# Residual products in three float32r passes instead of one float32 product

## The chip, the cores and the metric

The kernel runs on one core of one Trainium2 chip. The metric is the time of one execution on the device in microseconds, the median of several runs. Of the kernel before there are three: 1029.36, 1029.59 and 1030.19 us.

## What is computed

The reference takes the real part of a two-dimensional Fourier transform of every batch entry, normalises each row of the result, sends it through two dense layers with a ReLU between them, and adds the row back.

```python
X = np.fft.fft(x, axis=1)            # x: 8 x 3136 x 256
x = np.fft.fft(X, axis=2).real
mu = np.mean(x, axis=-1, keepdims=True)
var = np.mean((x - mu) ** 2, axis=-1, keepdims=True)
xn = (x - mu) / np.sqrt(var + 1e-06) * g_ln
ch = np.maximum(xn @ w_ch1, 0.0) @ w_ch2     # 256 -> 1024 -> 256
out = x + ch
```

All of it is float32. The row `x` that is added at the end is here called the residual.

## The kernel before, in words

The transform along the sequence is split into two steps. Step 1 (`step1`, L244 to L251) multiplies 64-point tables with folded input; its result goes through DRAM and comes back in another layout. Step 2 (`step2`, L298) multiplies that with tables of 98 or 99 columns and leaves in PSUM, for 196 or so frequencies, two sums of 128 rows each (`ps`, 128 x 2 x 196). A row of the transform is a product of these sums with a small table along the feature axis, and this last product is never made for the first dense layer: its table is multiplied into the weights at the start (`transform_w1`), so that the first dense layer works on step 2's sums.

Sums are collected in chunks of 256 frequencies, 49 chunks in all (0 to 48; the last one, `LC`, holds 264 columns). For each chunk step 2's evacuation makes three copies in SBUF:

- `ckh` (L318, ScalarE): the sums rounded to float32r, a format that TensorE multiplies in one pass;
- `ckl` (L322, VectorE): what the rounding left, also float32r;
- `ck` (L320, ScalarE): the sums as plain float32.

The letters of `step2`'s argument say which part runs: "m" the products, "h" the rounded copy, "f" the plain copy, "l" the rest.

A float32 product is then replaced by three float32r products: rest with rounded table, rounded data with the table's rest, rounded with rounded. The dense layers do this throughout (`moe1_a` L342, `moe2` L392). The residual does not: `residual` (L415) multiplies 128 columns of the plain copy `ck`, as the stationary operand, with the float32 table `ty_s` (two halves, of 129 and of 130 columns) into `psy`. That is two instructions to a tile of 128 frequencies and its mirror; there are two tiles to a chunk, four in the last, 100 in all. One tile of the last chunk needs a column set put together from both ends of the chunk (`mixed`, L402 to L404). ScalarE and VectorE then turn `psy` into rows `y` (L422 to L430), take their mean and variance (L437 to L458), and `finish` (L464, L466) adds the dense layers' result.

The main loop runs over s = 6 to 391, eight steps to a chunk. In every step stand, in this order: `moe1_b(s-1)` (ReLU and split, L356 and L357), `moe1_a(s)` (6 products, L342, then L347 to L349), the late list of the step, `moe2(s-3)` (12 products, L392), and the list `after[s]`, in which step 1, step 2 and the residual of chunk c (at s = 8c+5, for chunk 0 at s = 6) are put. The order on the four compute engines is the order in which the program is written; each engine takes its instructions in that order. `residual` writes into the two PSUM buffers `acc` that the chunk before used, so it follows the `finish` of that chunk.

Ahead of the loop stands a start-up part, in which the weights are unpacked from 64-bit numbers (L505 to L568) between the first steps 1 and 2, the tables of step 1 are split into `t1_hi` and `t1_lo`, and the first dense products are made.

Of the kernel before, what the change touches and what calls it, by code (L numbers as in the profile page):

```python
# [20 lines left out]
F32 = mybir.dt.float32  # L21
F32R = mybir.dt.float32r
# [3 lines left out]
ALU = mybir.AluOpType  # L26
# [6 lines left out]
CW = 256  # L33
NCH = -(-NB * REG // CW)
LC = NCH - 1
LASTR = NB * REG - LC * CW
MAXW = LASTR + 2 * NB
# [106 lines left out]
def tile_kernel(ctx: ExitStack, tc: tile.TileContext, x, g_ln, w1, w2, tu, tab, tz, ty, tw, out):  # L144
    nc = tc.nc
    const = ctx.enter_context(tc.tile_pool(name="const", bufs=1))
    work = ctx.enter_context(tc.tile_pool(name="work", bufs=2))
# [8 lines left out]
    tw_s = work.tile([128, 2, 2, 128], F32, tag="o", name="tw_s", bufs=3)  # L156
    ty_s = const.tile([128, 2, 130], F32, name="ty_s")
    g_s = const.tile([128, 2], F32, name="g_s")
    w1_hi = const.tile([128, 2, FF], F32R, name="w1_hi")
    w1_lo = const.tile([128, 2, FF], F32R, name="w1_lo")  # L160
    w2_hi = const.tile([128, 8, D], F32R, name="w2_hi")
# [5 lines left out]
    neg = const.tile([128, 1], F32, name="neg")  # L167
    single = const.tile([128, 2, 2 * NB], F32, name="single")
# [100 lines left out]
    chunk = {}  # L269

    def width(c):
        return MAXW if c == LC else CW

    def first_token(m):
        b, j = divmod(m, 8)
        return b * REG + max(gb[2 * j] - 2, 0)

    def singles():

        full, hi, lo = (t[:, :, LASTR:] for t in chunk[LC])  # L280
        nc.scalar.copy(full, single)
        nc.scalar.copy(hi, single)
        nc.vector.tensor_tensor(out=lo, in0=single, in1=hi.bitcast(F32), op=ALU.subtract)

# [3 lines left out]
    def step2(m, part, of=None):  # L288

        b, j = divmod(m, 8)  # L290
        base, end = gb[2 * j], gb[2 * j + 2]
        if "m" in part:
            ps2[m] = psum.tile([128, 2, CW], F32, tag="y" if m in second else "fft", name=f"ps2_{m}")
        ps = ps2[m]
        for g in (2 * j, 2 * j + 1) if "m" in part else ():
            k0, k1 = gb[g], gb[g + 1]
            for h in range(2):
                nc.tensor.matmul(ps[:, h, k0 - base:k1 - base], s2[b][:KP, g, 128 * h:128 * h + 128],  # L298
                                 tab_s[:, h, k0:k1], start=(h == 0 and g == 2 * j), stop=True,
                                 skip_group_check=True)  # L300
            if g == 0:
                nc.tensor.matmul(ps[:, 1, 0:50], zmu, tz_s, start=False, stop=True,
                                 skip_group_check=True)
        if j == 0 and "f" in part:
            nc.scalar.copy(single[:, :, 2 * b:2 * b + 2], ps[:, :, 0:2])
        t, stop = first_token(m), b * REG + end - 2
        while t < stop:
            c = t // CW
            n = min(stop, c * CW + CW) - t
            if c not in chunk:  # L310
                chunk[c] = (work.tile([128, 2, MAXW], F32, tag="ck", name=f"ck{c}", bufs=3),
                            work.tile([128, 2, MAXW], F32R, tag="ck_hi", name=f"ckh{c}", bufs=3),
                            work.tile([128, 2, MAXW], F32R, tag="ck_lo", name=f"ckl{c}", bufs=3))
            full, hi, lo = (x[:, :, t - c * CW:t - c * CW + n] for x in chunk[c])
            p0 = t - b * REG + 2 - base
            src = ps[:, :, p0:p0 + n]
            if "h" in part and of in (None, c):
                nc.scalar.copy(hi, src)  # L318
            if "f" in part:
                nc.scalar.copy(full, src)  # L320
            if "l" in part and of in (None, c):
                nc.vector.tensor_tensor(out=lo, in0=src, in1=hi.bitcast(F32), op=ALU.subtract)  # L322
            t += n

    PASSES = ((0, 1), (1, 0), (0, 0))
    hh = {}

    def moe1_a(s, passes=((0, 1), (1, 0), (0, 0))):
        c, f = divmod(s, 8)
        w = width(c)  # L330
        ch = chunk[c][1:]
        fs = slice(128 * f, 128 * f + 128)
        wt = (w1_hi, w1_lo)
        if w <= CW:
            ab = psum.tile([128, 2, CW], F32, tag="ab", name=f"ab{s}", bufs=2)
            pa, pb = ab[:, 0], ab[:, 1]
        else:
            pa = psum.tile([128, MAXW], F32, tag="ab", name=f"aa{s}", bufs=2)
            pb = psum.tile([128, MAXW], F32, tag="fft", name=f"bb{s}")
        for j, pt in ((0, pa), (1, pb)):  # L340
            for n, (wi, xi) in enumerate(passes):
                nc.tensor.matmul(pt, wt[wi][:, j, fs], ch[xi][:, j, :w],  # L342
                                 start=(n == 0), stop=(n == 2))
# [5 lines left out]
        nc.vector.tensor_tensor(out=h[:, w:], in0=asb[:, :m], in1=pb[:, :m], op=ALU.subtract)  # L349
# [32 lines left out]
    def moe2(s, halves=((0, 0), (0, 1), (1, 0), (1, 1))):  # L382

        c, f = divmod(s, 8)
        hs = hh[s]
        ws = (w2_hi, w2_lo)
        for i, side in halves:
            if f == 0 and side == 0:
                acc[c, i] = psum.tile([128, 2, D], F32, tag=f"acc{c % 2}", name=f"acc{c}_{i}", bufs=2)
            h0 = 256 * i + 128 * side if c == LC else 128 * i + 256 * side  # L390
            for n, (wi, xi) in enumerate(PASSES):
                nc.tensor.matmul(acc[c, i][:, side], hs[xi][:, h0:h0 + 128], ws[wi][:, f],  # L392
                                 start=(f == 0 and side == 0 and n == 0),
                                 stop=(f == 7 and n == 2), skip_group_check=True)
# [2 lines left out]

    def mixed():

        ck = chunk[LC][0]  # L400
        t = work.tile([128, 2, 128], F32, tag="asb", name="mixed")
        nc.scalar.copy(t[:, :, 0:8], ck[:, :, MAXW - 8:])  # L402
        nc.scalar.copy(t[:, 0, 8:], ck[:, 0, 0:120])
        nc.vector.tensor_scalar(out=t[:, 1, 8:], in0=ck[:, 1, 0:120], scalar1=neg, scalar2=None,  # L404
                                op0=ALU.mult)
        return t

    def residual(c, i):
        last = c == LC and i == 2
        ps = psum.tile([128, 2, 130], F32, tag="y" if last else f"acc{(c + 1) % 2}",  # L410
                       name=f"psy{c}_{i}", bufs=1 if last else 2)
        t0 = 120 if i == 3 else 128 * i
        ck = mixed() if last else chunk[c][0][:, :, t0:t0 + 128]
        for j in range(2):
            nc.tensor.matmul(ps[:, j, :129 + j], ck[:, j], ty_s[:, j, :129 + j],  # L415
                             start=(j == 0), stop=True, skip_group_check=True)
        res[c, i] = ps

    def residual_e(c, i):
# [103 lines left out]
    def split(hi, lo, src, eng=nc.vector):  # L523
        nc.scalar.copy(hi, src)
        eng.tensor_tensor(out=lo, in0=src, in1=hi.bitcast(F32), op=ALU.subtract)
# [55 lines left out]
    def add(s, fn, *args):  # L581

        after.setdefault(s, []).append((fn, args))

    def add_late(s, fn, *args):

        late.setdefault(s, []).append((fn, args))

    first = {}
    for m in range(3, 64):  # L590
        s = 8 * (first_token(m) // CW) - 3
# [2 lines left out]
        first.setdefault(s, []).append(m)  # L594
    for s, ms in first.items():
        for m in ms:
            add(s, step2, m, "mhf")
        for m in ms:
            add_late(s + 1, step2, m, "l")
    for b in range(1, NB):  # L600
# [17 lines left out]
    for c in range(LC):  # L618
        s = 8 * c + (5 if c else 6)
# [26 lines left out]
    with tc.manual_schedule(engines={E.PE, E.Activation, E.DVE, E.Pool}):  # L646
        with tc.manual_schedule(engines={E.SP}):
# [70 lines left out]
            for i in range(NU):  # L718
# [5 lines left out]
            f = finish_w2(0)  # L724
# [5 lines left out]
            step2(1, "m")  # L730
            step2(1, "hl", 0)
            moe1_a(0, ((1, 0), (0, 0), (0, 1)))
            step2(0, "f")
            convert_a("w2_1", w2p[1])
            moe1_a(1, ((1, 0), (0, 0), (0, 1)))
            convert_b("w2_1")
# [8 lines left out]
            step2(1, "f")  # L745
            step2(1, "hl", 1)
            moe2(0)
            convert_a("w2_2", w2p[2])
# [5 lines left out]
            f = finish_w2(2)  # L754
# [3 lines left out]
            moe1_a(5)  # L758
            moe1_b(4)
            convert_b("w2_3")  # L760
            step2(2, "hf")
            step2(2, "l")
            moe2(2)
            split(t1_hi, t1_lo, tu_s[:, 0:128])
            add_late(6, make_w2, 3)

        main.append(True)
        lag, last = 3, 8 * NCH
# [33 lines left out]
```

## Time and profile before

| what | value |
|---|---|
| median of three runs | 1029.59 us |
| the profiled execution's own time | 1029.71 us |
| its span in the trace | 1027.9 us |
| mean granted TensorE clock | 0.997 |
| TensorE busy | 1008.6 us, 98% of the span |
| VectorE busy | 816.0 us, 79% |
| ScalarE busy | 539.7 us, 53% |
| GpSimd busy | 245.0 us, 24% |

The span is the stretch between the first and the last instruction of the trace; 1.8 us of the execution's time lie around it. Names of tiles are printed without buffer numbers. A float32 product stands in the trace as two pairs of a weight load (PEld) and a matmul (PE), a float32r product as one such pair. The shape behind a matmul is rows x moving columns; "128*128" is the stationary tile. In the timeline a row is start, duration, engine, line and operation, and like instructions that follow each other are merged ("x8"). Matmuls overlap in the pipeline, so the distance between starts, not the duration, says what one costs.

### The profile page before, as it was taken

What the parts mean: (1) busy time and instruction counts of PE and PEld (TensorE: products, weight loads), DVE (VectorE), ACT (ScalarE), POOL (GpSimd) and SP (SyncE); (2) the same over time, 40 slices, a digit from 0 to 9 for tenths busy, and PEclk for the clock granted to TensorE, in tenths of its full rate; (3) what the DMA queues carried; (4) which work ended last, traced back from release to release, by engine and by line L of the source; (5) the groups of instructions that cost most, each with busy time, mean ns of one, the idle gap of its engine ahead of it and who ended that gap; (6) DMA issues with size and microseconds to landing.
All of it is one profiled execution on the core that took longest, in us unless ns stands there. A gap on an engine that the chain in (4) does not pass through costs nothing.

```text
span 1027.9 us, 21753 instructions
## 1 busy us (share of the span) xinstructions
PE 1008.6 (98%) x8282; PEld 986.0 (96%) x8283; DVE 816.0 (79%) x2195; ACT 539.7 (53%) x1410; POOL 245.0 (24%) x277
## 2 busy tenths in 40 slices
PE   9799999999999999999999999999999999999997
PEld 6489999999999999999999999999999999999997
DVE  5788787778878878887887887878788778788787
ACT  2445555554465555555455545654555554455553
POOL 1146503440135202532034401442024300000000
PEclk9999999999999999999999999999999999999999
DMA  9923341423222331234114132223101230100101
GB/s 332 263 98 128 109 134 52 135 83 103 66 99 87 108 94 42 94 102 135 43 62 144 63 103 82 84 93 114 62 24 51 73 103 22 42 22 21 42 22 42
DMA packets 41528, 92.04 MB, mean 90 GB/s; under 512 B 4176, under 2 KB 18704, under 8 KB 40528
## 3 DMA queue, kind: packets, MB, share of 16 engines
q1 hardware_dynamic: 40016, 88.81, 26.4%
q8 instruction: 66, 1.08, 0.5%
q0 software_dynamic: 320, 1.05, 0.3%
q10 hardware_dynamic: 1088, 0.79, 0.2%
q14 instruction: 38, 0.31, 0.1%
HBM read 50.26 MB, written 40.37 MB: 88 GB/s over the span
## 4 chain that ended last, share of the span: by engine, by line
PE 93%; DVE 5%; ACT 1%; issue 0%; DVEq 0%; ACTq 0%
PE acc L392 51%; PE ab L342 26%; PE ps L298 5%; PE psy L415 4%; PE ps L251 3%; DVE h_lo L357 1%; PE pw L643 1%; DVE h L348 1%; DVE h L349 1%; PE ps L244 1%; PE ps L246 1%; ACT h_hi L356 0%; DVE ew L520 0%; PE psw L558 0%; DVE fw L507 0%
## 5 line engine op out<-in xcount | busy, mean ns | idle before, releaser
L392 PE MATMUL acc<-w_hi,h_lo 128*128 128x256 f32 x1568 | 438.9, 280 | 2.8 <-DVE h_lo L357 2.8
L392 PE MATMUL acc<-w_hi,h_hi 128*128 128x256 f32 x1568 | 439.1, 280 | 0.0
L392 PE MATMUL acc<-w_lo,h_hi 128*128 128x256 f32 x1568 | 438.8, 280 | 0.0
L357 DVE SCALAR_TENSOR_TENSOR h_lo<-h,h_hi 128x512 fp32r<-128x512 f32 x392 | 287.9, 735 | 174.1 <-ACT h_hi L356 172.3
L356 ACT ACTIVATE h_hi<-h 128x512 fp32r<-128x512 f32 x392 | 249.8, 637 | 254.2 <-DVE h L349 253.9
L392 PEld LDWEIGHTS acc<-w_hi,h_lo 128*128 128x128 f32 x1568 | 295.6, 189 | 3.3 <-DVE h_lo L357 3.2
L392 PEld LDWEIGHTS acc<-w_lo,h_hi 128*128 128x128 f32 x1568 | 295.5, 188 | 0.0
L392 PEld LDWEIGHTS acc<-w_hi,h_hi 128*128 128x128 f32 x1568 | 295.4, 188 | 0.0
L342 PE MATMUL ab<-ckl,w_hi 128*128 128x256 f32 x768 | 220.9, 288 | 3.7 <-DVE h L349 3.7
L342 PE MATMUL ab<-ckh,w_lo 128*128 128x256 f32 x768 | 216.0, 281 | 0.4 <-ACT ckh L318 0.4
L342 PE MATMUL ab<-ckh,w_hi 128*128 128x256 f32 x768 | 214.8, 280 | 0.0
L214 POOL TENSOR_TENSOR fl<-f,fh 128x512 fp32r<-128x512 f32 x49 | 64.8, 1321 | 506.9 <-ACT fh L208 506.9
L348 DVE TENSOR_TENSOR h<-asb,ab 128x256 f32<-128x256 f32 x384 | 158.8, 414 | 2.2 <-ACT asb L347 2.2
L349 DVE TENSOR_TENSOR h<-asb,ab 128x256 f32<-128x256 f32 x384 | 158.9, 414 | 0.0
L342 PEld LDWEIGHTS ab<-ckl,w_hi 128*128 128x128 f32 x768 | 144.5, 188 | 7.2 <-ACT ye L423 1.7
L347 ACT COPY asb<-ab 128x256 f32<-128x256 f32 x384 | 139.3, 363 | 18.7 <-PE ab L342 12.9
L342 PEld LDWEIGHTS ab<-ckh,w_lo 128*128 128x128 f32 x768 | 145.0, 189 | 2.6 <-ACT ckh L318 0.5
L342 PEld LDWEIGHTS ab<-ckh,w_hi 128*128 128x128 f32 x768 | 145.1, 189 | 0.0
L254 ACT COPY s<-ps 128x508 f32<-128x508 f32 x56 | 32.7, 585 | 82.9 <-PE ps L251 65.4
L318 ACT CAST ckh<-ps 128x392 fp32r<-128x392 f32 (+49 forms) x112 | 39.6, 355 | 66.0 <-PE ps L298 65.7
L298 PE MATMUL ps<-tab_s,s 112*128 112x98 f32 (+1 forms) x512 | 66.4, 275 | 0.1
L298 PEld LDWEIGHTS ps<-tab_s,s 112*128 112x128 f32 x512 | 63.0, 194 | 0.6 <-PE pw L643 0.6
(108 smaller groups left out, 964.9 us busy)
## 6 DMA issues: line engine op xcount, KB each, us to landing
xs<-x SPq DMA_DIRECT2D x56, 512.0 KB, 4.6
out<-o SPq DMA_DIRECT2D x96, 256.0 KB, 3.0
scratch<-s SPq DMA_DIRECT2D x49, 256.0 KB, 2.2
s<-scratch SPq DMA_DIRECT2D x7, 1792.0 KB, 9.9
w1p_all<-w SPq DMA_DIRECT2D x8, 512.0 KB, 8.7
scratch<-s POOLq DMA_DIRECT2D x4, 256.0 KB, 6.0
s<-scratch SPq DMA_DIRECT2D x2, 448.0 KB, 5.9
s<-scratch SPq DMA_DIRECT2D x1, 896.0 KB, 11.7
```

What stands on the lines that cost most here:

```text
L214: nc.gpsimd.tensor_tensor(out=lo, in0=f, in1=hi.bitcast(F32), op=ALU.subtract)
L254: nc.scalar.copy(s[:, :, :, :127], ps[:, :, :, :127])
L298: nc.tensor.matmul(ps[:, h, k0 - base:k1 - base], s2[b][:KP, g, 128 * h:128 * h + 128], tab_s[:, h, k0:k1], start=(h == 0 and g == 2 * j), ...
L318: nc.scalar.copy(hi, src)
L342: nc.tensor.matmul(pt, wt[wi][:, j, fs], ch[xi][:, j, :w], start=(n == 0), stop=(n == 2))
L347: nc.scalar.copy(asb[:, :w], pa)
L348: nc.vector.tensor_tensor(out=h[:, :w], in0=asb[:, :w], in1=pb, op=ALU.add)
L349: nc.vector.tensor_tensor(out=h[:, w:], in0=asb[:, :m], in1=pb[:, :m], op=ALU.subtract)
L356: nc.scalar.activation(h_hi, h, AF.Relu)
L357: nc.vector.scalar_tensor_tensor(out=h_lo, in0=h, scalar=0.0, in1=h_hi.bitcast(F32), op0=ALU.max, op1=ALU.subtract)
L392: nc.tensor.matmul(acc[c, i][:, side], hs[xi][:, h0:h0 + 128], ws[wi][:, f], start=(f == 0 and side == 0 and n == 0), stop=(f == 7 and n = ...
L415: nc.tensor.matmul(ps[:, j, :129 + j], ck[:, j], ty_s[:, j, :129 + j], start=(j == 0), stop=True, skip_group_check=True)
```

## The change

The residual's product is made as the dense layers make theirs: the table `ty_s` is split once into `ty_hi` and `ty_lo`, and each half of each tile is multiplied in three float32r passes from `ckl` and `ckh`. Both halves now have 130 columns. The plain copy `ck` is no longer made: all "f" parts of `step2` go, 112 ScalarE copies, one more in `singles`, and a pool of three buffers. `mixed` now builds a rounded and a remaining tile, with twice the copies. In the start-up part one `split` of the table is added.

```diff
+    ty_hi = const.tile([128, 2, 130], F32R, name="ty_hi")
+    ty_lo = const.tile([128, 2, 130], F32R, name="ty_lo")
...
     def singles():
-        full, hi, lo = (t[:, :, LASTR:] for t in chunk[LC])
-        nc.scalar.copy(full, single)
+        hi, lo = (t[:, :, LASTR:] for t in chunk[LC])
...
             if "h" in part and of in (None, c):
                 nc.scalar.copy(hi, src)
-            if "f" in part:
-                nc.scalar.copy(full, src)
...
     def mixed():
-        ck = chunk[LC][0]
-        t = work.tile([128, 2, 128], F32, tag="asb", name="mixed")
-        nc.scalar.copy(t[:, :, 0:8], ck[:, :, MAXW - 8:])
-        nc.scalar.copy(t[:, 0, 8:], ck[:, 0, 0:120])
-        nc.vector.tensor_scalar(out=t[:, 1, 8:], in0=ck[:, 1, 0:120], scalar1=neg, scalar2=None,
-                                op0=ALU.mult)
-        return t
+        out = []
+        for ck, tag in zip(chunk[LC], ("f_hi", "f_lo")):
+            t = work.tile([128, 2, 128], F32R, tag=tag, name=f"mixed_{tag}")
+            nc.scalar.copy(t[:, :, 0:8], ck[:, :, MAXW - 8:].bitcast(F32))
+            nc.scalar.copy(t[:, 0, 8:], ck[:, 0, 0:120].bitcast(F32))
+            nc.vector.tensor_scalar(out=t[:, 1, 8:], in0=ck[:, 1, 0:120].bitcast(F32), scalar1=neg,
+                                    scalar2=None, op0=ALU.mult)
+            out.append(t)
+        return out
...
     def residual(c, i):
-        ck = mixed() if last else chunk[c][0][:, :, t0:t0 + 128]
+        ck = mixed() if last else [x[:, :, t0:t0 + 128] for x in chunk[c]]
         for j in range(2):
-            nc.tensor.matmul(ps[:, j, :129 + j], ck[:, j], ty_s[:, j, :129 + j],
-                             start=(j == 0), stop=True, skip_group_check=True)
+            for n, (ti, xi) in enumerate(PASSES):
+                nc.tensor.matmul(ps[:, j], ck[xi][:, j], (ty_hi, ty_lo)[ti][:, j],
+                                 start=(j == 0 and n == 0), stop=(n == 2), skip_group_check=True)
...
-            add(s, step2, m, "mhf")
+            add(s, step2, m, "mh")
...
-            step2(2, "hf")
+            step2(2, "h")
             step2(2, "l")
             moe2(2)
+            split(ty_hi, ty_lo, ty_s)
             split(t1_hi, t1_lo, tu_s[:, 0:128])
```

`PASSES` is ((0, 1), (1, 0), (0, 0)), pairs of table and data with 0 for rounded and 1 for the rest. What the change does to the order on the engines is seen at three places.

On TensorE, the residual of chunk 1 before (`ps_3` is step 2, `psy_0` and `psy_1` are the two tiles, `ab` is the first dense layer of the next step):

```order
L298 MATMUL ps_3_814<-tab_s,s_0_260 128x98 x4
L415 MATMUL psy_0_827<-ty_s,ck_335 128x129
L415 MATMUL psy_0_827<-ty_s,ck_335 128x130
L415 MATMUL psy_1_830<-ty_s,ck_335 128x129
L415 MATMUL psy_1_830<-ty_s,ck_335 128x130
L342 MATMUL ab_837<-ckl_337,w_hi 128x256
```

The same place now, from step 2 to the first product of the second tile (line numbers of the changed file):

```order
L299 MATMUL ps_3_818<-tab_s,s_0_262 128x98 x4
L416 MATMUL psy_0_828<-ty_hi,ckl_338 128x130
L416 MATMUL psy_0_828<-ty_lo,ckh_337 128x130
L416 MATMUL psy_0_828<-ty_hi,ckh_337 128x130
L416 MATMUL psy_0_828<-ty_hi,ckl_338 128x130
L416 MATMUL psy_0_828<-ty_lo,ckh_337 128x130
L416 MATMUL psy_0_828<-ty_hi,ckh_337 128x130
L416 MATMUL psy_1_835<-ty_hi,ckl_338 128x130
```

Two instructions of a tile have become six, at the same place between step 2 and the dense products.

On VectorE, the end of the start-up part before (`ckl` is the rest of step 2's sums, `t_lo` the rest of step 1's table, `h_lo` the ReLU's rest in step 6):

```order
L520 SCALAR_TENSOR_TENSOR ew_3_479<-w1p_all,ew_3_479 128x512
L322 TENSOR_TENSOR ckl_337<-ps_2_456,ckh_336 128x2x121
L322 TENSOR_TENSOR ckl_463<-ps_2_456,ckh_462 128x2x75
L525 TENSOR_TENSOR t_lo<-tu_s,t_hi 128x128
L357 SCALAR_TENSOR_TENSOR h_lo_525<-h_493,h_hi_524 128x512
```

and now:

```order
L521 SCALAR_TENSOR_TENSOR ew_3_475<-w1p_all,ew_3_475 128x512
L320 TENSOR_TENSOR ckl_338<-ps_2_453,ckh_337 128x2x121
L320 TENSOR_TENSOR ckl_459<-ps_2_453,ckh_458 128x2x75
L526 TENSOR_TENSOR ty_lo<-ty_s,ty_hi 128x260
L526 TENSOR_TENSOR t_lo<-tu_s,t_hi 128x128
L355 SCALAR_TENSOR_TENSOR h_lo_521<-h_489,h_hi_520 128x512
```

One operation of 260 columns, `ty_lo`, has come in ahead of `t_lo`; the residual of chunk 0 reads it.

On ScalarE, the evacuation of two steps 2 that feed chunks 3 and 4, before (`ckh` the rounded, `ck` the plain copy, `h_hi` the ReLU of the next step):

```order
L318 CAST ckh_822<-ps_4_1148 128x2x196
L320 COPY ck_821<-ps_4_1148 128x2x196
L318 CAST ckh_822<-ps_5_1155 128x2x45
L320 COPY ck_821<-ps_5_1155 128x2x45
L318 CAST ckh_1163<-ps_5_1155 128x2x151
L320 COPY ck_1162<-ps_5_1155 128x2x151
L356 ACTIVATE h_hi_1174<-h_1132 128x512
```

and now:

```order
L345 COPY asb_1140<-ab_1133 128x256
L318 CAST ckh_824<-ps_4_1157 128x2x196
L318 CAST ckh_824<-ps_5_1163 128x2x45
L318 CAST ckh_1169<-ps_5_1163 128x2x151
L354 ACTIVATE h_hi_1187<-h_1141 128x512
```

The three plain copies are gone, and the ReLU follows the last rounded copy.

More of the change, by code (lines that the diff above doesn't have):

```diff
@@ L303, in step2 @@
                                  skip_group_check=True)
-        if j == 0 and "f" in part:
+        if j == 0 and "h" in part:
             nc.scalar.copy(single[:, :, 2 * b:2 * b + 2], ps[:, :, 0:2])
@@ L310, in step2 @@
             if c not in chunk:
-                chunk[c] = (work.tile([128, 2, MAXW], F32, tag="ck", name=f"ck{c}", bufs=3),
-                            work.tile([128, 2, MAXW], F32R, tag="ck_hi", name=f"ckh{c}", bufs=3),
+                chunk[c] = (work.tile([128, 2, MAXW], F32R, tag="ck_hi", name=f"ckh{c}", bufs=3),
                             work.tile([128, 2, MAXW], F32R, tag="ck_lo", name=f"ckl{c}", bufs=3))
-            full, hi, lo = (x[:, :, t - c * CW:t - c * CW + n] for x in chunk[c])
+            hi, lo = (x[:, :, t - c * CW:t - c * CW + n] for x in chunk[c])
             p0 = t - b * REG + 2 - base
@@ L330, in moe1_a @@
         w = width(c)
-        ch = chunk[c][1:]
+        ch = chunk[c]
         fs = slice(128 * f, 128 * f + 128)
@@ L732, in tile_kernel @@
             moe1_a(0, ((1, 0), (0, 0), (0, 1)))
-            step2(0, "f")
             convert_a("w2_1", w2p[1])
@@ L744, in tile_kernel @@
             moe1_a(3)
-            step2(1, "f")
             step2(1, "hl", 1)
```

## Prediction

> **What bounds the kernel now.** I began with the page: busy time of each engine, then the chain that ended last.
>
> ```profile
> PE 1008.6 (98%) x8282; PEld 986.0 (96%) x8283; DVE 816.0 (79%) x2195; ACT 539.7 (53%) x1410; POOL 245.0 (24%) x277
> ...
> PE 93%; DVE 5%; ACT 1%; issue 0%; DVEq 0%; ACTq 0%
> ```
>
> TensorE is busy for 98% of the span, and 93% of the chain lies on it. Next come the waits of TensorE over the whole run: who held it up, the total in microseconds, how often, and the longest.
>
> ```profile
> PE ab L342 <- DVE h L349: 3.7, 6, 1.5
> ...
> PE ab L342 <- ACT ckh L318: 0.4, 1, 0.4
> ```
>
> The longest total is 3.7 us, and ScalarE is named once, with 0.4. Hardly any of it lies in the body of the run: from 83 to 993 us, by the table of windows, TensorE is busy for 908.94 of 910 us, against 730.71 on VectorE and 491.79 on ScalarE.
>
> ```profile
> 83.00:993.00 910.00, 908.94 (x7654) 902.35 (x7654) 730.71 (x1992) 491.79 (x1289) 224.90 (x246) 1.00 0.25 80
> ```
>
> So in the body of the run each stretch that the change adds to TensorE is paid in full, and what it takes from ScalarE is paid out nowhere, unless TensorE waits for ScalarE there. The question is what a residual tile costs on TensorE in six narrow float32r pairs instead of four narrow float32 pairs. A pair is a weight load and a matmul; matmuls overlap in the pipeline, so a duration isn't a price, and I go by distances between starts. The timeline of the weight loads around the residual of one chunk (two tiles, eight loads) has them:
>
> ```profile
> 401.94 0.97 PEld L415 LDWEIGHTS psy<-ty_s,ck 128*128 128x128 f32 x8
> 402.83 0.19 PEld L342 LDWEIGHTS ab<-ckl,w_hi 128*128 128x128 f32 x1
> 402.94 0.19 PEld L342 LDWEIGHTS ab<-ckh,w_lo 128*128 128x128 f32 x1
> ```
>
> Eight pairs take 402.83 - 401.94 = 0.89 us, 0.111 us each, and a tile of four pairs 0.445 us.
>
> **What a narrow float32r pair will cost.** No row of this trace has a float32r product of fewer than 256 columns, so the price is bounded from both sides. First the moving columns. The chain shows the 18 dense pairs of a step, float32r with 256 columns; the timeline shows step 1's products with 512 (fl, fh):
>
> ```profile
> 98.15 0.71 PE ab L342 x6
> 98.86 1.42 PE acc L392 x12
> ```
>
> ```profile
> 409.95 0.39 PE L251 MATMUL ps<-fl,t_hi 128*128 128x512 f32 x1
> 410.18 0.39 PE L251 MATMUL ps<-fh,t_lo 128*128 128x512 f32 x1
> ```
>
> 256 columns take (0.71 + 1.42)/18 = 0.118 us, 512 take 410.18 - 409.95 = 0.23: the time goes with the columns. For 130 that makes 130/256 x 0.118 = 0.060 us. That is the low end, if columns alone count. Now the loads. Here are the products of step 1's ends, float32, with 14 moving columns (L226, L227) or a single one (L230):
>
> ```profile
> 407.07 0.30 PEld L226 LDWEIGHTS pse<-e0c,tu_s 128*128 128x128 f32 x2
> 407.29 0.30 PEld L227 LDWEIGHTS pse<-e0c,tu_s 128*128 128x128 f32 x2
> 407.52 0.28 PEld L230 LDWEIGHTS pse<-one,masked 128*112 128x112 f32 x2
> 407.71 0.19 PEld L342 LDWEIGHTS ab<-ckl,w_hi 128*128 128x128 f32 x1
> ```
>
> Two loads with 14 columns behind them take 0.22 us, as long as two with 129. With 112 stationary columns instead of 128 two take 0.19. So in a row of narrow products it is the weight load that sets the pace, at 0.11 us for 128 stationary columns, however few columns move. For float32r there are two places where a load isn't held back by a wide matmul ahead of it: the first load of `ab` after the residual, 402.83 to 402.94, 0.11 us, and the warm-up's first two:
>
> ```profile
> 7.22 0.19 PEld L643 LDWEIGHTS pw<-warm_r 128*128 128x128 f32 x1 [0.89 <-PE pw L643]
> ...
> 7.33 0.19 PEld L643 LDWEIGHTS pw<-warm_r 128*128 128x128 f32 x1
> ```
>
> Again 0.11. A float32r load therefore costs what a float32 load does, and I take 0.111 us for the pair: the load's pace, not the columns' 0.060. The nearest float32r pairs, of 256 columns, give 0.118 as the upper end of this case.
>
> **The change part by part.**
>
> *Six pairs instead of four.* Two more pairs of 0.111 us are 0.222 us a tile. (That the first half gains a 130th column changes nothing at this pace.) There are 100 tiles, and for four of them it is not all on the path. Chunk 0's two stand in the start-up stretch, and chunk 1's first tile ahead of a wait of TensorE:
>
> ```profile
> 58.36 1.05 PE L415 MATMUL psy<-ty_s,ck 128*128 128x129 f32 x8
> ...
> 80.63 0.71 PE L415 MATMUL psy<-ty_s,ck 128*128 128x129 f32 x4 [1.63 <-DVE o L466]
> ```
>
> What comes ahead of 80.63 has 1.63 us of wait to spare there. The fourth is the tile from `mixed`, below. The other 96 are paid in full: 96 x 0.222 = 21.3 us. With 0.109 and 0.118 for a pair (the first is 0.002 less, what two decimals of such distances leave open) the ends are 96 x (0.654 - 0.445) = 20.1 and 96 x (0.708 - 0.445) = 25.2.
>
> *The wait for ty_lo.* The residual of chunk 0 will need the table's rest, which VectorE makes late, ahead of `t_lo`:
>
> ```profile
> 60.25 0.28 DVE L525 TENSOR_TENSOR t_lo<-tu_s,t_hi 128x128 fp32r<-128x128 f32 x1
> 60.45 0.69 DVE L357 SCALAR_TENSOR_TENSOR h_lo<-h,h_hi 128x512 fp32r<-128x512 f32 x1
> ```
>
> 128 columns take 0.20 us there from start to start; an estimate for 260 is 0.3, between that and the 0.69 that the 512 columns of the second row last. VectorE leads the chain in this stretch, so 0.3 us goes on the path. TensorE stood at this product at 58.36 and will now wait, after its first pair, until about 60.6. Queued behind are the 11 other pairs (1.2 us) and the dense products of the next step (0.71 for `ab`, 1.42 for `acc`, as above), which end at 63.9 instead of 58.36 + 0.89 + 0.71 + 1.42 = 61.4: 2.5 us late. The waits that TensorE has between 60 and 82 us are the cover:
>
> ```profile
> PE ab L342 <- DVE h L349: 2.3, 4, 1.5
> PE psy L415 <- DVE o L466: 1.6, 1, 1.6
> ```
>
> They make 3.9 us, more than 2.5. I cost the stall at nothing; if that cover weren't there, for example because VectorE in turn waits for the late `ab`, it would be up to 2.5 us.
>
> *The plain copies go.* 112 copies leave ScalarE, 40.3 us:
>
> ```profile
> L320 ACT COPY ck<-ps 128x392 f32<-128x392 f32 (+49 forms) x112 | 40.3, 364 | 0.0
> ```
>
> In the body this meets a wait of TensorE once. The chain between 80 and 130 us shows it: copies, ReLU, and the rest `ckl` one after another, then step 1's product, which waits for the last `ckl`; the timeline has that wait.
>
> ```profile
> 101.18 0.49 ACT ckh L318
> 101.67 0.39 ACT ck L320
> 102.45 0.31 ACT ckh L318
> 102.76 0.32 ACT ck L320
> ...
> 104.99 1.02 DVE ckl L322 x3
> ```
>
> ```profile
> 106.15 0.48 PE L251 MATMUL ps<-fl,t_hi 128*128 128x512 f32 x1 [1.06 <-DVE ckl L322]
> ```
>
> Two plain copies are 0.39 + 0.32 = 0.7 us of it, and chunk 2's residual, which runs on TensorE beside them, takes 0.44 us of the wait as well. Together that is the whole 1.1 us: -1.1. Everywhere else the copies are hidden behind TensorE already, and they bring nothing.
>
> *The tail.* `mixed` gets two more ScalarE copies and one more VectorE operation, and TensorE waits there already:
>
> ```profile
> 1002.45 0.40 PE L415 MATMUL psy<-ty_s,mixed 128*128 128x129 f32 x2
> 1003.28 0.49 PE L415 MATMUL psy<-ty_s,mixed 128*128 128x130 f32 x2 [0.43 <-DVE mixed L404]
> ```
>
> The second operation takes 0.2 us (`t_lo`'s start to start), and of the two new pairs one, of the second half, comes after it: 0.1. Together 0.3. The last `ck` copy in `singles` goes: 0.1 less.
>
> *Sum.* 21.3 + 0.3 - 1.1 + 0.3 - 0.1 = 20.7 us. The profiled execution took 1029.71 us, 1.8 above its span and 0.12 above the median of the three; on it this makes 1050.4. A difference of 0.2%, 2 us, is about what a measurement of this kernel can tell from none.
>
> **The rivals.**
>
> *The load is not the limit (faster).* If float32r pairs of 130 columns ran at their columns' pace, a tile would take 6 x 0.060 = 0.36 us instead of 0.445, and 96 tiles would give 8.2 us back: 1020.9 with the other terms (-0.6). The point at which this decides is a pair of 0.445/6 = 0.074 us: below it the change gains. For it: loads overlap, with 0.19 us of duration every 0.11. Against it: the rows with 14 columns and with one, which would have run far below 0.11 if columns counted. Chance 0.05. Just at 0.074 nothing changes (within 0.2%): 0.02.
>
> *The load is hidden in part.* A pair halfway between, at 0.085 us, makes 0.51 us a tile, 0.065 more: 6 us, 1035.4. Against it the same rows, all at 0.11. Chance 0.04. The Trainium skill (TensorE: Matmul & The Clock Gate, "Back-to-back issue gap") gives about 81 ns for each pair in a sustained stream with 128 moving columns; by that rule the time would be an estimate of 1033 us. The loads of this trace, 0.11 us apart with 14 columns, so far speak against it for four-byte operands.
>
> *Narrow float32r takes more passes.* Nothing here shows float32r below 256 columns, and it could need several passes of its columns. Two passes are 0.12, the upper end above. Four are 0.24 us a pair, 1.44 a tile, 0.995 more: 96 tiles make 95.5 us, 1124.6 with the other terms. It decides from about 0.12 on, where columns overtake the load. For it speaks only that this program has no such product; against it, that the time went with the columns from 256 to 512 without a step. Chance 0.09.
>
> *As forecast*, with the load's pace: 0.80.
>
> **Numbers.** The likeliest case gives 1050.4 us. Its ends are 1029.7 + 20.1 - 1.1 - 0.1 = 1048.6 and 1029.7 + 25.2 + 0.6 = 1055.5; I go to 1047.5 below, since the plain copies' end might be worth another microsecond in the start-up stretch. The range 1047.5 to 1055.5 leaves out the rivals at 1021, 1035 and 1125 us, 2 in 10 in all. Faster 0.05, same 0.02, slower 0.93 (0.80 + 0.09 + 0.04).
>
> **What the profile of the changed kernel would show.** Twelve loads of `psy` to a chunk in 1.33 us, 0.111 from start to start, and 200 more matmuls and loads on the page. TensorE's share stays at 98%; ScalarE's busy time falls by some 40 us, to about 500. At 58 us `psy` waits about 2 us for `ty_lo`, and the wait at 80.6 nearly vanishes. No wait for `ckl` is left at 106. The forecast is wrong if `psy`'s loads stand at 0.06 to 0.09 us or the matmuls at 0.24, or if the loss comes from new waits instead of from twelve loads.

## The result, and the profile after

The kernel after takes 1054.57 us (median of six runs, 1054.15 to 1056.30), the kernel before beside it 1029.89 us (six runs, 1029.36 to 1031.58). The ratio is 1.0238, with a 95% interval of 1.0225 to 1.0252. The direction and the mechanism came as forecast, and the time lies inside the range; it is 4.2 us above the 1050.4 that was held likeliest. The profiled execution took 1054.17 us, 24.46 more than that of before, where the steps summed to 20.7. So there are 20 us to confirm, and 3.8 us to find.

The page of the kernel after, its busy times, its granted clock in 40 slices and its chain:

```profile
PE 1034.8 (98%) x8482; PEld 1012.3 (96%) x8483; DVE 818.8 (78%) x2197; ACT 509.8 (48%) x1300; POOL 243.7 (23%) x277
...
PEclk9989999999999999999999999999999999999999
...
PE 94%; DVE 5%; ACT 1%; issue 0%; ACTq 0%; DVEq 0%
```

There are 200 more matmuls and 200 more loads, as expected, and TensorE stays at 98%. ScalarE falls by 29.9 us (539.7 to 509.8), not by the 40 expected: the 40.3 us were the sum of the durations of 112 copies, and durations of instructions that follow each other closely overlap, so the busy time on the page loses less than the group's row shows. Nobody waited for ScalarE, so this costs the forecast nothing. New is the 8 in the third slice of the clock (53 to 79 us).

The timeline of the weight loads of the kernel after, around the residual of one chunk (twelve loads of `psy`, then the first of `ab`):

```profile
410.72 0.19 PEld L416 LDWEIGHTS psy<-ty_hi,ckl 128*128 128x128 f32 x1
410.83 0.19 PEld L416 LDWEIGHTS psy<-ty_lo,ckh 128*128 128x128 f32 x1
...
411.95 0.19 PEld L416 LDWEIGHTS psy<-ty_hi,ckh 128*128 128x128 f32 x1
412.06 0.19 PEld L340 LDWEIGHTS ab<-ckl,w_hi 128*128 128x128 f32 x1
```

From 410.72 to 412.06 are 1.34 us for twelve, 0.112 each (forecast 1.33 and 0.111). Eight loads took 0.89 before. That is 0.45 us a chunk.

To see where the other microseconds lie, I compare the starts of the same products in both traces: one in step 0, the first `ab` of step 15, and the first `aa` of the last chunk (step 384). The timeline of the matmuls before:

```profile
40.19 0.36 PE L342 MATMUL ab<-ckl,w_hi 128*128 128x256 f32 x1
...
83.28 0.28 PE L342 MATMUL ab<-ckl,w_hi 128*128 128x256 f32 x1
...
998.07 0.28 PE L342 MATMUL aa<-ckl,w_hi 128*128 128x264 f32 x1
```

The same three in the timeline after:

```profile
40.69 0.36 PE L340 MATMUL ab<-ckl,w_hi 128*128 128x256 f32 x1
...
85.07 0.28 PE L340 MATMUL ab<-ckl,w_hi 128*128 128x256 f32 x1
...
1021.71 0.28 PE L340 MATMUL aa<-ckl,w_hi 128*128 128x264 f32 x1
```

The distances grow from 0.50 to 1.79, 23.64 and, at the end, 24.46 us. By stretch, with the terms of the forecast sorted into the same stretches:

| stretch | forecast | measured |
|---|---|---|
| to step 0 | 0 | 0.50 |
| step 0 to 15 | 0.3 + 0.22 = 0.5 | 1.29 |
| step 15 to 384, residuals of 46 chunks | 92 x 0.222 - 1.1 = 19.3 | 21.85 |
| from there to the end | 3 x 0.222 + 0.3 - 0.1 = 0.9 | 0.82 |
| sum | 20.7 | 24.46 |

The first 0.50 us lie ahead of everything that the change touches: nearly all of them are there already in the first eight products of zeros with which TensorE warms up. The chain before, and then after:

```profile
1.49 5.69 PE pw L643 x8
```

```profile
1.49 6.18 PE pw L644 x8
```

Two stretches remain, with 0.8 and 2.5 us.

**Step 0 to 15.** The waits of TensorE over the whole run after:

```profile
PE psy L416 <- DVE ty_lo L526: 2.1, 1, 2.1
...
PE psy L416 <- DVE o L467: 1.5, 2, 1.2
PE ps L253 <- DVE ckl L320: 1.0, 1, 1.0
PE ab L340 <- DVE h L347: 0.8, 1, 0.8
```

The wait for `ty_lo` is there, 2.1 us. The waits for `h` shrank from 3.7 to 0.8 us and those for `o` from 3.0 to 1.5: they are the cover on which the forecast counted, and they are used up. The timeline of the matmuls after shows why they did not suffice:

```profile
58.87 0.22 PE L416 MATMUL psy<-ty_hi,ckl 128*128 128x130 f32 x1
61.20 0.47 PE L416 MATMUL psy<-ty_lo,ckh 128*128 128x130 f32 x1 [2.11 <-DVE ty_lo L526]
61.48 0.41 PE L416 MATMUL psy<-ty_hi,ckh 128*128 128x130 f32 x1
61.69 0.41 PE L416 MATMUL psy<-ty_hi,ckl 128*128 128x130 f32 x1
```

After the wait the pairs stand 0.21 us apart, not 0.11. The table of windows after, where the column ahead of the DMA share and the GB/s is the granted clock:

```profile
62.00:66.00 4.00, 4.00 (x20) 4.00 (x20) 2.78 (x5) 1.83 (x5) 1.99 (x2) 0.50 0.00 0
66.00:70.00 4.00, 4.00 (x29) 4.00 (x28) 2.38 (x7) 1.62 (x6) 3.91 (x6) 0.76 0.35 117
```

And the same table before:

```profile
62.00:66.00 4.00, 2.47 (x20) 2.30 (x21) 2.43 (x4) 2.58 (x8) 2.79 (x4) 1.00 0.00 0
```

In these four microseconds TensorE starts as many matmuls as before, 20, but is busy for 4.00 us instead of 2.47, at a clock of 0.50.

**Step 15 to 384.** The wait at 106 us, which the forecast let vanish with the plain copies (-1.1), is still there: 0.99 us at 108.27. The chain of the kernel after at that place:

```profile
102.02 1.76 PE ps L299 x16
103.78 1.32 PE psy L416 x12
105.10 0.78 PE ab L340 x6
...
105.96 0.38 ACT asb L345
...
106.36 0.42 DVE h L346
106.78 0.33 DVE h L347
107.11 1.02 DVE ckl L320 x3
...
108.27 0.93 PE ps L253 x3
```

Before, the copies of ScalarE stood between `ps` and `ckl` in the chain. Now the chain reaches `ckl` by way of `h` on VectorE, and the input of `h`, `ab`, is made by TensorE itself, after the residual: TensorE waits for work that its own longer residual has put back. The rest of the stretch, 2.55 - 1.1 = 1.4 us, has no wait beside it. It lies in the dense products: twelve loads of `moe2` take a mean of 1.4016 us before and 1.4075 after, from the starts of the first load of a group and the one that follows its last, over all groups between 120 and 985 us, at a granted clock of 1.00 in both.

### The profile page after: what moved, and what is told of

It is laid out like the page before. It is cut to its first block, busy times and chain, and to the rows that moved or that the text cites. A ratio compares the mean times of both kernels' runs of the same rounds, so it can differ in the third digit from the quotient of the medians.

```text
span 1052.4 us, 22045 instructions
## 1 busy us (share of the span) xinstructions
PE 1034.8 (98%) x8482; PEld 1012.3 (96%) x8483; DVE 818.8 (78%) x2197; ACT 509.8 (48%) x1300; POOL 243.7 (23%) x277
## 4 chain that ended last, share of the span: by engine, by line
PE 94%; DVE 5%; ACT 1%; issue 0%; ACTq 0%; DVEq 0%
PE acc L390 50%; PE ab L340 25%; PE psy L416 6%; PE ps L299 5%; PE ps L253 3%; PE pw L644 1%; DVE h_lo L355 1%; DVE h L346 1%; DVE h L347 1%; PE ps L246 1%; PE ps L248 0%; DVE ew L521 0%; PE psw L559 0%; DVE fw L508 0%; ACT asb L345 0%
## 5 line engine op out<-in xcount | busy, mean ns | idle before, releaser
L318 ACT CAST ckh<-ps 128x392 fp32r<-128x392 f32 (+49 forms) x112 | 34.2, 350 | 72.1 <-PE ps L299 72.1
```

## The experiments

**Theory.** In a row of narrow products the weight load sets the pace, 0.111 us for 128 stationary columns whatever moves; a float32r pass of the residual costs that, and everything else is small change (the clock after the wait for `ty_lo`, the copies). **First rival:** the moving columns, or the float32r passes over them, set the price. **Second rival:** a good part of the loss comes from the new wait for `ty_lo` with its half clock, so that an early table gives it back. Ratios below are to the kernel before, on the same chip.

### Half the moving columns

The second and third pass move 64 columns instead of 130.

```diff
-                nc.tensor.matmul(ps[:, j], ck[xi][:, j], (ty_hi, ty_lo)[ti][:, j],
+                k = 130 if n == 0 else 64
+                nc.tensor.matmul(ps[:, j, :k], ck[xi][:, j], (ty_hi, ty_lo)[ti][:, j, :k],
```

> The changed kernel with the second and third pass of each product made for the first 64 of the 130 moving columns only; the other columns keep the first pass alone. Theory (the weight load sets the pace of a pair): loads of psy stay 0.111 us apart, 1054 us, within 1 us of the changed kernel. Rival (moving columns count): 66 columns less at 0.118/256 us each are 0.030 us a pair, four such pairs to a tile, 98 tiles: 12 us less, 1042.

It took 1054.35 us (1052.34 to 1056.13), ratio 1.0235 (1.0214 to 1.0256). The loads of a chunk in its timeline, the first of `psy` and the first of `ab` behind it:

```profile
411.03 0.19 PEld L417 LDWEIGHTS psy<-ty_hi,ckl 128*128 128x128 f32 x1
...
412.37 0.19 PEld L340 LDWEIGHTS ab<-ckl,w_hi 128*128 128x128 f32 x1
```

Still 1.34 us for twelve. The moving columns cost nothing here, and the first rival is out. The Trainium skill (TensorE: Matmul & The Clock Gate, "Back-to-back issue gap") gives about 81 ns for a pair in a stream with 128 moving columns; this trace has 112 with 130 and with 64, and differs.

### Half the stationary columns

The same two passes load 64 stationary columns instead of 128.

```diff
-                nc.tensor.matmul(ps[:, j], ck[xi][:, j], (ty_hi, ty_lo)[ti][:, j],
+                k = 128 if n == 0 else 64
+                nc.tensor.matmul(ps[:k, j], ck[xi][:, j, :k], (ty_hi, ty_lo)[ti][:, j],
```

> The changed kernel with the second and third pass of each product made for 64 of the 128 stationary columns only; the other rows of the tile keep the first pass alone. Theory (the time to load stationary columns sets the pace): 16 columns less were worth 0.016 us on the products of step 1's ends, so 64 columns load in about 0.05 us, and the 130 moving columns, 0.06 us, become the limit: four pairs of a tile save 0.05 us each, 98 tiles, 20 us less, 1034. Rival (a fixed price for each pair, however much is loaded): no change, 1054.

It took 1033.18 us (1032.68 to 1035.75), ratio 1.0039 (1.0025 to 1.0054). Its loads, with the stationary columns as the second number of 128*64:

```profile
402.54 0.19 PEld L417 LDWEIGHTS psy<-ty_hi,ckl 128*128 128x128 f32 x1
402.65 0.14 PEld L417 LDWEIGHTS psy<-ty_lo,ckh 128*64 128x64 f32 x1
402.71 0.14 PEld L417 LDWEIGHTS psy<-ty_hi,ckh 128*64 128x64 f32 x1
402.78 0.19 PEld L417 LDWEIGHTS psy<-ty_hi,ckl 128*128 128x128 f32 x1
...
403.48 0.19 PEld L340 LDWEIGHTS ab<-ckl,w_hi 128*128 128x128 f32 x1
```

A pass with half the load costs 0.06 us, one with the whole 0.11, and the chunk 0.94 instead of 1.34. The same number of products, with the same 130 moving columns, is 21.4 us faster than the kernel after (1054.57 - 1033.18), most of the loss. The price goes with the stationary columns, and a fixed price for each pair is out. What half a load costs by itself the run doesn't show: its 0.06 us are also what the prediction estimated for 130 moving columns (0.060). (The Trainium skill, same page, "LDWEIGHTS (loading the stationary operand)", lets a load grow with its columns, at 1.2 columns a nanosecond. By it the two loads would take 107 and 53 ns; the 0.11 agrees, and the 0.06 is an upper bound for the second.)

### Two passes

The pass of the data's rest with the rounded table is left out.

```diff
-            for n, (ti, xi) in enumerate(PASSES):
+            for n, (ti, xi) in enumerate(PASSES[1:]):
...
-                                 start=(j == 0 and n == 0), stop=(n == 2), skip_group_check=True)
+                                 start=(j == 0 and n == 0), stop=(n == 1), skip_group_check=True)
```

> The changed kernel without the first of the three passes (the rest of the data with the rounded table): four float32r pairs to a tile where the kernel before had four float32 pairs. Theory (a pair costs the load of 128 stationary columns, whatever its type): the time of the kernel before plus what the start-up part keeps, 0.6 us without and 1.4 us with a drop of the clock there: 1030 to 1031.5, within 0.2% of the kernel before in the same call. Rival (float32r pairs have a price of their own, for example a larger one for narrow products): 4 pairs x 98 tiles x the difference, 4 us or more for each 0.01 us.

It took 1032.22 us (1030.38 to 1033.40), ratio 1.0016 (1.0005 to 1.0028), 0.7 above the upper edge of what was expected. Eight loads of float32r with the plain copies gone take 0.89 us a chunk, the same as the eight of the float32 product before: two passes of float32r cost what one float32 product costs. The ten executions fall apart by the mean clock that was granted to each: the six at 0.993 or 0.994 have a median of 1032.6 us, the four at 0.997 one of 1030.6. The profiled one is of the first kind, with a clock of 0.62 from 62 to 66 us, after a wait for `ty_lo` of 2.2 us.

### One load for two passes

If the load is the price, a pass that shares a load should be nearly free. Here the rounded data is loaded once for 256 moving columns, 130 of the rounded table and 126 of its rest, and the data's rest once for 130. The table is split early. The sums with the table's rest land in columns of their own and aren't added.

```diff
...
-                nc.tensor.matmul(ps[:, j], ck[xi][:, j], (ty_hi, ty_lo)[ti][:, j],
-                                 start=(j == 0 and n == 0), stop=(n == 2), skip_group_check=True)
+            nc.tensor.matmul(ps[:, j], ck[0][:, j], ty_both[:, j],
+                             start=(j == 0), stop=False, skip_group_check=True)
+            nc.tensor.matmul(ps[:, j, :130], ck[1][:, j], ty_hi[:, j],
+                             start=False, stop=True, skip_group_check=True)
```

> The three products with one load of the rounded data less: the rounded table and 126 columns of its rest stand side by side, and the rounded data, loaded once, is multiplied with all 256 columns; the rest of the data follows with 130 columns. The sums with the table's rest stand in columns of their own and are not added, so two additions to a tile are left out. The split stands early, as in the kernel with the early split. Theory (price by loads, or by columns where they are more): a tile is 2 x 0.118 + 2 x 0.111 = 0.458 us against 0.445 before, 98 tiles make 1.3 us, with the start-up part's 0.6 about 2 us above the kernel before, 1031.5 to 1032.5, and some 21 us below the changed kernel. Rival (a price for each of the three products, however loaded): no better than the changed kernel, 1053.

It took 1032.28 us (1031.97 to 1035.02), ratio 1.0027 (1.0014 to 1.0041), as expected. All three products of a tile are made (of the table's rest 126 of 130 columns), with eight loads to a chunk; its timeline:

```profile
402.61 0.19 PEld L415 LDWEIGHTS psy<-ty_both,ckh 128*128 128x128 f32 x1
402.73 0.19 PEld L417 LDWEIGHTS psy<-ty_both,ckl 128*128 128x128 f32 x1
...
403.54 0.19 PEld L340 LDWEIGHTS ab<-ckl,w_hi 128*128 128x128 f32 x1
```

0.93 us a chunk: of two passes that share a load the second costs (0.93 - 0.89)/4 = 0.01 us.

### The table split early

The split of the table is moved ahead of the late start-up work, its rest made on GpSimd.

```diff
             moe1_b(3)
+            split(ty_hi, ty_lo, ty_s, nc.gpsimd)
...
-            split(ty_hi, ty_lo, ty_s)
             split(t1_hi, t1_lo, tu_s[:, 0:128])
```

> The changed kernel, but the table's split stands some 8 us earlier in the start-up part, and its rest is made on GpSimd, which is idle there. Nothing waits for ty_lo then. Theory: the wait of 2.1 us at 59 us in the changed kernel also brought the granted clock down to half from 62 to 68 us, and the dense products of that stretch ran at 0.213 us a pair; both go. 1.0 to 1.5 us less than the changed kernel, about 1053.2, a clock of 1.00 in all windows from 58 to 82 us, and a wait of psy at about 81 us again. Rival: the cover of 3.9 us absorbs the stall as the prediction had it: no gain beyond the 0.3 us of the VectorE operation, 1054.2.

It took 1052.88 us (1052.45 to 1053.31), ratio 1.0221 (1.0206 to 1.0237): 1.7 us less than the kernel after, a little more than the theory's 1.0 to 1.5. The wait for `ty_lo` is gone, the clock from 58 to 82 us is 1.00, and the loss is 22.5 us (1052.88 against 1030.41 for the kernel before beside it) instead of 24.7; in its profile the growth from step 0 to 15 is 0.74 us instead of 1.29, by the starts 40.21 and 84.04 of the same two products. So the early table gains 0.55 us there; of the 1.03 us between the two profiled executions the other 0.48 lie ahead of step 0, which is another matter. The 0.74 are still more than the 0.22 that the forecast had for this stretch without `ty_lo` on VectorE: the chain of this run goes over the twelve loads of chunk 0's residual (1.29 us from 59.13), whose four added pairs the forecast had left off the path. The second rival is a small matter: most of the loss is there without wait or half clock.

### A busy wait

Ten bf16 products of zeros are put where TensorE waits for `ty_lo`, so that it waits working.

```diff
...
+            if s == 6:
+                warm_up(10, warm_h, "y")
```

> The changed kernel with ten bf16 products of zeros on TensorE (0.215 us each) ahead of the residual of chunk 0, so that TensorE is busy for most of the 2.1 us in which it waited for ty_lo. Theory (the idle time, together with where it falls in the clock's own window, brings the half clock): no half clock between 58 and 82 us, the residual's pairs at 0.111 us there, and about 0.5 to 1 us less than the changed kernel: 1053.3 to 1054. Rival (the half clock has nothing to do with the wait): it is seen again in that stretch, 1054.2 or more.

It took 1053.86 us (1052.53 to 1055.20), ratio 1.0230 (1.0208 to 1.0251). The time is too near to that of the kernel after to say that it helped; the clock speaks more plainly. The windows of this run:

```profile
62.00:66.00 4.00, 4.00 (x36) 4.00 (x36) 2.78 (x6) 2.26 (x7) 1.82 (x2) 1.00 0.00 0
...
82.00:90.00 8.00, 8.00 (x57) 8.00 (x57) 6.11 (x16) 4.42 (x15) 3.85 (x5) 0.79 0.30 98
```

and of the two passes, whose wait is idle:

```profile
62.00:66.00 4.00, 4.00 (x24) 4.00 (x24) 2.78 (x6) 2.32 (x7) 1.83 (x2) 0.62 0.00 0
...
82.00:90.00 8.00, 8.00 (x57) 8.00 (x57) 6.37 (x16) 4.59 (x15) 4.24 (x5) 0.79 0.30 98
```

With the wait filled the half clock after it is missing, and 36 matmuls pass where 24 did. Up to the wait the two executions are alike: both were granted 0.79 from 34 to 42 us and 0.90 from 54 to 58. The later one, behind the wait for `o` at 81 us, which neither fills, stands in both at the same place and with the same 0.79. In these two executions an idle stretch of TensorE of 1.4 to 2.2 us is thus followed by some microseconds of half clock, and a filled one isn't.

### The plain copies kept

The residual runs in three passes, but the plain copies are made as before, and nothing reads them.

```diff
...
+            if "f" in part:
+                nc.scalar.copy(full, src)
```

> The changed kernel with the plain copies still made on ScalarE, in the places that they had before; nothing reads them. Theory: ScalarE is off the path everywhere, the copies' removal gave nothing: within 0.7 us of the changed kernel, 1053.9 to 1055.3, and the wait at about 108 us stays at about 1 us in both. Rival: the removal gave back the 0.7 to 1.1 us that the prediction counted, or more: 1055.5 to 1057.

It took 1053.84 us (1052.88 to 1054.22), ratio 1.0229 (1.0213 to 1.0246), just below the 1053.9 at which the expectation began, and not slower than the kernel after. Two of its four executions had a mean clock of 0.993, like four of the six of the kernel after, and at that clock the times agree: 1054.08 and 1054.22 here, 1054.15, 1054.17, 1054.27 and 1056.30 there. Its group of copies is back, and so is the wait of TensorE for `ckl` of 1.0 us; the window at 62 us has all of its clock:

```profile
L322 ACT COPY ck<-ps 128x392 f32<-128x392 f32 (+49 forms) x112 | 40.3, 364 | 0.0
```

```profile
62.00:66.00 4.00, 4.00 (x36) 4.00 (x36) 2.78 (x5) 2.26 (x7) 2.43 (x4) 1.00 0.00 0
```

So 40.3 us of ScalarE's work were worth nothing, not even the 1.1 us that I gave them. This run tells a second thing. It has the wait for `ty_lo`, 2.1 us, but no half clock after it, and the growth from step 0 to 15 is 0.58 us, by the starts 40.24 and 83.91 of the same two products: here the cover held, as the forecast had it (0.5). The stall by itself was costed rightly; the half clock, in the executions that have it, is what was missing.

### The data's rest in bf16

If the price is the load, a cheaper load would be a way to a faster version. The rest is copied to bf16 once a chunk on ScalarE, and its pass uses a bf16 table; the table is split early.

```diff
...
+        t = lob[c] = work.tile([128, 2, MAXW], BF16, tag="ck_b", name=f"ckb{c}")
+        nc.scalar.copy(t[:, :, :width(c)], chunk[c][1][:, :, :width(c)].bitcast(F32))
...
-                nc.tensor.matmul(ps[:, j], ck[xi][:, j], (ty_hi, ty_lo)[ti][:, j],
+                nc.tensor.matmul(ps[:, j], ck[xi][:, j], (ty_b if xi else (ty_hi, ty_lo)[ti])[:, j],
```

> The kernel with the early split, but the pass of the data's rest is made in bf16: ScalarE copies the rest of each chunk to bf16 (one copy to a chunk), and the table has a bf16 copy. It tells whether a load's price goes with the type. The trace of the kernel before has bf16 loads of 0.10 us where float32r loads last 0.19, and bf16 products of 512 columns 0.215 us apart, 0.055 for 130. Theory: the bf16 pair isn't paced by its load at 0.111; at about 0.06 us a tile takes 4 x 0.111 + 2 x 0.06 = 0.565 us instead of 0.667, 98 tiles 10 us less than with the early split: 1043. Rival (128 columns load in 0.111 us in any type): no change, 1053.

It took 1047.15 us (1046.79 to 1049.41), ratio 1.0170 (1.0147 to 1.0194): between the two forecasts. Its loads:

```profile
408.17 0.19 PEld L424 LDWEIGHTS psy<-ty_hi,ckh 128*128 128x128 f32 x1
408.34 0.10 PEld L424 LDWEIGHTS <-ckb 128*128 128x128 bf16 x1
408.35 0.20 PEld L424 LDWEIGHTS psy<-ty_lo,ckh 128*128 128x128 f32 x1
408.47 0.19 PEld L424 LDWEIGHTS psy<-ty_hi,ckh 128*128 128x128 f32 x1
```

The load after the bf16 one comes only 0.01 us behind it, but the bf16 one itself comes 0.17 us after its forerunner. The three passes take 0.30 us together (408.17 to 408.47), 0.03 less than three of float32r.

### Shared load and bf16 rest together

Both ways together, with VectorE adding the two parts of the sum; nothing of the reference is left out.

```diff
...
+            nc.tensor.matmul(ps[:, j], ck[0][:, j], ty_w[:, j],
+                             start=(j == 0), stop=False, skip_group_check=True)
+            nc.tensor.matmul(ps[:, j, :130], ck[1][:, j], ty_b[:, j],
+                             start=False, stop=True, skip_group_check=True)
...
+        nc.vector.tensor_tensor(out=inner, in0=inner,
+                                in1=ps[:, :, 130:].rearrange("p j (b k) -> p j b k", b=2), op=ALU.add)
```

> What the runs point to: one float32r load of the rounded data for the rounded table and its rest side by side (256 columns; the rest has 126, the others are exactly zero), and the data's rest in bf16. VectorE adds the two parts, one operation more to a tile; nothing is left out. Theory: a tile is 2 x 0.118 + 2 x 0.06 = 0.356 us against 0.445 before: 98 tiles give 8.7 us, and the start-up part takes about 1 us: 1022, faster than the kernel before. Rivals: bf16 loads cost 0.111 too, 0.458 us a tile, 1032; or the extra operation on VectorE (some 0.4 us a tile, 40 us) comes on the path, near 1030 or above.

It took 1055.96 us (1053.32 to 1056.36), ratio 1.0243 (1.0222 to 1.0264); the forecast of a gain failed, on both of its steps. First the loads, by its timeline:

```profile
409.35 0.19 PEld L422 LDWEIGHTS psy<-ty_w,ckh 128*128 128x128 f32 x1
409.58 0.10 PEld L424 LDWEIGHTS <-ckb 128*128 128x128 bf16 x1
409.58 0.20 PEld L422 LDWEIGHTS psy<-ty_w,ckh 128*128 128x128 f32 x1
```

The bf16 load comes 0.23 us after the load for 256 columns; four such pairs of passes make 0.97 us a chunk, more than the 0.89 before. Second, VectorE's additional work is not hidden. It is more than the one operation to a tile that was expected: besides the 100 additions of 408 ns (40.8 us) the two operations that make `y` now add the bias in ScalarE's place, and take 91.2 us instead of 56.0. The waits of TensorE in this run:

```profile
PE ab L341 <- DVE h L348: 12.1, 19, 1.5
```

These operations stand ahead of `h` in VectorE's queue, and TensorE waits for `h` 19 times, 12.1 us in all, where the kernel before has 6 waits and 3.7 us. No version here beats the kernel before: with early tables and eight loads the residual would cost what it does now (the shared load), and the sum over its two parts has then still to be made.

## Why the prediction was right, and where it was short

- *Six pairs instead of four, 0.222 us a tile, 21.3 us.* Right, in size and in cause: 1.34 us for twelve loads, unchanged with half the moving columns, down to 0.94 with half the stationary ones. The rows with 14 and with one moving column in the trace of before told it. The 0.111 us that they gave for float32 held for float32r.
- *The wait for ty_lo, +0.3 us, the stall under cover.* `ty_lo` took 0.33 us, the wait was 2.1, and in the run with the plain copies kept the cover held: 0.58 us of growth for 0.5. What failed is that the step took the clock after the wait as granted. In the profiled execution, as in those of three kernels with changed passes that wait as long (0.50 with half the moving columns, 0.63 with half the stationary ones, 0.62 with two passes, each over the window of 4 us where it is lowest), clock was withheld behind it; 1.29 us of growth instead of 0.5. The trace of before could have warned of it: TensorE waits 2.2 us for `h_lo` up to 49.4 us there, and the windows then show a clock of 0.59:

```profile
50.00:54.00 4.00, 4.00 (x23) 4.00 (x23) 3.86 (x8) 0.65 (x2) 0.00 (x0) 0.59 1.03 410
```

- *The plain copies go, -1.1 us.* This step failed. The wait at 106 us is 0.99 us after, and 1.0 with the copies kept. The step read the chain as a row of copies on ScalarE and let the wait shrink by what was taken out of them. But the last `ckl` also stands behind `h` on VectorE, and `h` waits for TensorE's `ab`, which comes after the residual. When one of two paths to a wait becomes shorter, the other sets its end. The longer residual moved that other path by 0.44 us as well, so it could not eat into the wait, as the step had it.
- *The body, step 15 to 384,* is 1.4 us above its sum beyond that. The dense groups of `moe2` are 0.006 us longer each in the kernels with three passes and without plain copies (1.4075 us a group; 1.4074 with two passes, so it isn't the passes), and 1.4043 with the plain copies kept. Over the 368 groups of these 46 chunks 0.006 us makes 2.2 us, more than enough. Why they are longer isn't settled: the clock is 1.00, no wait stands beside them, and the medians with and without the copies don't differ enough to tell.
- *The tail, +0.87 us* with its three other tiles: 0.82.
- *The 0.50 us ahead of step 0* are no part of the change: the first eight products of zeros took 6.18 us instead of 5.69 in that execution. The kernel before by itself took from 1027.3 to 1031.8 us in the other runs.
- *The rivals.* The load as no limit (1020.9), the load hidden in part (1035.4) and several passes of the columns (1124.6) are all excluded by the 0.112 us that stayed 0.112 with half the columns.

Of the 3.8 us between forecast and profiled execution, 0.5 are a difference between executions, 0.8 the clock, 1.1 the wait that stayed, and 1.4 are open.

## What to carry to other kernels

Narrow products are paid by their weight loads: count stationary columns loaded, not moving columns, and a float32 product of two such loads is cheaper than three float32r passes that load each time. This ends where the moving columns take longer than the load. Step 1's first products are float32 with 256 moving columns, and on the chain of before one of them, two pairs, takes 0.43 us:

```profile
16.01 0.43 PE ps L246 x2
```

Three float32r pairs of 256 columns take 3 x 0.118 = 0.35 us, and there the split pays. Where a trace has products of the same stationary width with far fewer moving columns, their spacing tells this before the change is made. A copy that is taken off an engine is worth only what the next path to the same wait leaves, so follow that second path back too: here it led to the very engine that was waiting.

## What the runs showed of the hardware that was not expected

- Behind an idle stretch of TensorE of about 2 us the granted clock fell for some microseconds, to 0.50 to 0.63 as a mean over 4 us, in the kernel after and in the three with changed passes, but not with the plain copies kept, whose wait was as long. In the kernel before, waits of 1.5 and 1.6 us between 62 and 82 us are followed by a clock of 1.00; what decides it isn't settled here. The Trainium skill (TensorE: Matmul & The Clock Gate, Part 1) describes a window of about 3.4 us that runs freely, with half clock until a window has been busy; that the same wait is punished in one execution and not in another agrees with it. By its section "HAM oscillation — how this bites in real kernels" the gap to avoid is one over some 3.4 us; here 2.1 us were enough, and the measurement decides.
- The time of one kernel goes with this clock from execution to execution: with half of the stationary columns in two passes, five executions at a mean clock of 0.997 have a median of 1032.8 us, three at 0.993 one of 1035.6. Differences of 2 to 3 us between kernels of this kind need the clock beside them.
- A bf16 load between float32r products doesn't keep the 0.11 us of a float32r load: it came 0.17 us after the load of a pair with 130 columns and 0.23 after one with 256, and the next float32r load 0.01 us behind it.
